# Attention and gated FFN on one core: the last six sections with their loads, splits and gates in another order

## Chip, cores and metric

One core of a Trainium2 chip runs the whole kernel. The metric is the device time of one execution in microseconds (us); a shorter time is better. Times of the profile are counted from the start of the span, which is the time from the first to the last instruction.

## What is computed

A block with attention and a gated FFN on the same normalised input, cut to what matters:

```python
x  = A_x                                  # 1 x 2048 x 576
xn = layernorm(x)
s  = attention(xn, wqkv, 32 heads) @ wo   # the "o" projection comes last
g  = silu((gelu(xn @ w_gate) * (xn @ w_up)) @ w_down)   # hidden size 4608
return x + s * g
```

All data is float32. A product keeps its accuracy by splitting an operand into a high part (rounded to the type that TensorE multiplies fast) and a low part (what is left), so each product is done three times: high by high, high by low, low by high. Making the parts is called a split here.

## The kernel before

**The work.** Tokens are cut into four blocks of 512 (`NB`). The FFN runs block by block in sections: a section makes one chunk of 128 hidden values for the 512 tokens of a block. It multiplies the gate and up weights of the chunk (`gate_up`, L417, 54 matmuls with 512 columns), applies the activation on ScalarE and VectorE, and splits the hidden values (`finish`). Two sections (`G = 2`) share one tile of down weights; after the second of a pair the down weights are split too (`dh`, `dl`), and the two sections that follow each do half of the down products (`down`, L466, 24 matmuls with 288 columns) and add them to Y on VectorE (`add_down`, L455). There are 144 sections; sections 10 to 137 run beside attention. The diff touches the last six, the loop at the end with `n` from 128 to 133. A section is named by this n below.

**The places.** While the last six sections run, the output of attention is projected. A place is 128 tokens (16 places, four to a block). `prepare(p)` splits its normalised attention output (`split_o` on GpSimd, L108, L110, L887) and asks for its rows of `x` and of the stored FFN sum `ys` (`load_xy`, L896 and L898). `load_o` (L876, L877) fetches a block of attention output (1152 KB) into one of two tiles `OT`. `gate_place` makes the silu gate of a place (`gate`: tanh on ScalarE, L424, and one operation on VectorE, L425). `project_o` (L907) makes two products of 14 matmuls, and `put` (L914, L915) multiplies them by the gate, adds `x`, and stores the row of the output (L918). Each of the sections 129 to 132 does three places; two more are projected in section 133 and the last two at the end. For the FFN the last block is finished by `final`.

**What sets the order.** TensorE's order is written out by hand. From the last six sections on, `FF["keep"]` is true and `kept` holds nearly every other instruction to the order in which the program issues it on its engine: VectorE, ScalarE, GpSimd and SP (which starts all DMAs) each run a queue in order, and an instruction that waits holds up what stands behind it. PSUM has three banks under the tag "s"; the products of a section (four of the down sums, six of the places) take them in turn, so a product waits until VectorE has read the product three before it. The rows `xx` and `yy` have four buffers each; while the attention output of the last two heads' groups still has to be normalised (`load_numbers`, `norm_numbers`, L593 to L599), one of the four holds its numbers.

**The loads of weights.** `section` asks for the gate and up weights of the section that follows (`load_gu`, L128) and splits them on GpSimd in three pieces (`split_gu`, tiles `wh`, `wl`, L108 and L110): two before its own products, one behind them in the order of the program. The down weights (L553) are asked for in the second section of a pair, the one whose `finish` splits them on ScalarE (`dh`, L118) and VectorE (`dl`, L119).

Of the kernel before, what the change touches and what calls it, by code (L numbers as in the profile page):

```python
# [8 lines left out]
F32 = mybir.dt.float32  # L9
# [8 lines left out]
P = 128  # L18
NT = S // P
TB = 512  # L20
# [18 lines left out]
G = 2  # L39
# [30 lines left out]
def kernel(ctx: ExitStack, tc: tile.TileContext, x, wqkv, wo, w_gate, w_up, w_down, out):  # L70
# [50 lines left out]
    def raw_tile(shape, pool=wts):  # L121
        return pool.tile(shape, F32, name="raw", tag="raw", bufs=2)
# [278 lines left out]
    def kept(i):  # L401

        if FF["keep"]:
            tc.keep_in_program_order(i)
        return i
# [121 lines left out]
            for j in js:  # L527
                kept(nc.sync.dma_start(ys[b * TB + j * P:b * TB + (j + 1) * P, :], Y[:, j]))

    def section(specials=(), tag="f", raw_d=None):  # L530

        n = FF["n"]
        FF["n"] += 1
        b, r = divmod(n // G, NR)
        g = n % G
        pairs, pg, pu = gate_up(tag)
        if g == 0:
            FF["hs"] = []
        keep = kept
        if asked:  # L540
            xd_last = asked.pop()

            def keep(i):
                no_sync(i, xd_last, "transposed x first")
        nxt = load_gu((n + 1) % (NR * G), keep) if n + 1 < NF else None
        if nxt:
            for k in range(NG - 1):
                first = split_gu(nxt, k, kept)
                if k == 0 and n in ATT and n > ATT.start:
                    no_sync(first, FF["hl"], "hidden values first")  # L550
        if g == G - 1:
            raw = FF["rawd"] = raw_d() if raw_d else raw_tile([P, G, D])
            kept(nc.sync.dma_start(raw, w_down[r * G * P:(r + 1) * G * P, :].rearrange("(g p) n -> p g n", p=P)))  # L553
        for p in spread(pairs, specials):
            p()
        if nxt:
            split_gu(nxt, NG - 1, kept)
        FF["w"] = nxt
        if n + 1 < NF and (n + 1) % (NR * G) == 0:
            FF["xd"] = load_xd(b + 1, FF["key"])  # L560
        FF["act"], FF["rest"] = activate(pg, pu, n < ATT.stop)
        if n < ATT.stop and (n not in ATT or g or not FF["down"] or not FF["down"][0][-2]):
            run_rest()
# [299 lines left out]
    with tc.tile_pool(name="epi", bufs=1, reuse_waits="tile") as epi:  # L863
        AHEAD = 3
        OL = [epi.tile([P, NK, P], F32R, name=f"ol{i}") for i in range(AHEAD)]
        OT = [epi.tile([P, NK, TB], F32, name=f"OT{i}") for i in range(2)]
        OH = [epi.tile([P, NK, P], F32R, name=f"oh{i}") for i in range(AHEAD)]
        S2 = epi.tile([P, 2, D], F32, name="S2")
        OUT = [(k, x, w) for k in range(KT) for x, w in ((0, 0), (0, 1), (1, 0))] + [(KT, 0, 0), (KT, 0, 1)]
        ENDS = NF - len(FIRST)  # L870
        XY = {}

        def load_o(b):

            toks = slice(b * TB, (b + 1) * TB)
            kept(nc.sync.dma_start(OT[b % 2][:, 0:KT, :], oN[0:R0, toks].rearrange("(k p) t -> p k t", p=P)))  # L876
            kept(nc.sync.dma_start(OT[b % 2][0:HR, KT, :], oN[R0:D, toks]))  # L877

        def parts_of(b, j):
            i = (b * TB // P + j) % AHEAD  # L880
            return OH[i], OL[i]

        def split_o(b, j):

            oh, ol = parts_of(b, j)
            split(oh, ol, OT[b % 2][:, :, j * P:(j + 1) * P], kept)
            kept(nc.gpsimd.tensor_copy(oh[HR:P, KT, :], ol[0:HR, KT, :]))  # L887

        def row_tile(name):
            return epi.tile([P, D], F32, name=name, bufs=AHEAD + 1)  # L890

        def load_xy(b, j):

            rows = slice(b * TB + j * P, b * TB + (j + 1) * P)
            xx, yy = XY[b, j] = row_tile("xx"), row_tile("yy")
            kept(nc.sync.dma_start(xx, x[rows, :]))  # L896
            if b < NB - 1:
                kept(nc.sync.dma_start(yy, ys[rows, :]))  # L898

        def gate_place(b, j):  # L900
            yy = XY[b, j][1]
            gate(yy, epi.tile([P, D], F32, name="th"), yy)

        def project_o(b, j, c, tag):
            po = ps.tile([P, TB], F32, name="po", tag=tag, bufs=BANKS[tag])[:, 0:288]
            for i, (k, x_, w) in enumerate(OUT):
                nc.tensor.matmul(po, parts_of(b, j)[x_][:, k, :], OW[w][c][k], start=(i == 0), stop=(i == len(OUT) - 1))  # L907
            return po

        def put(b, j, c, po, add):  # L910

            cc = slice(288 * c, 288 * c + 288)
            xx, yy = XY[b, j]
            kept(nc.vector.scalar_tensor_tensor(yy[:, cc], yy[:, cc], 0.25, po, op0=ALU.mult, op1=ALU.mult))  # L914
            kept(add.tensor_tensor(yy[:, cc], yy[:, cc], xx[:, cc], op=ALU.add))  # L915
            if c or b == NB - 1:
                cc = cc if b == NB - 1 else slice(0, D)
                kept(nc.sync.dma_start(out[b * TB + j * P:b * TB + (j + 1) * P, cc], yy[:, cc]))  # L918

        def cut(hi, lo, raw):  # L920
            split_av(hi, lo, raw, kept)

        places = [(b, j) for b in range(NB) for j in range(TB // P)]

        def prepare(p):

            if p < len(places):
                b, j = places[p]
                split_o(b, j)
                if j == TB // P - 1 and b + 2 < NB:  # L930
                    load_o(b + 2)
                load_xy(b, j)

        for o in OT:
            nc.gpsimd.memset(o[HR:P, KT, :], 0.0)
        load_o(0)
        done = 0
        for n in range(NU * NA, ENDS):
            last = n == ENDS - 1
            section([], "m" if n % 2 else "f",  # L940
                    (lambda: epi.tile([P, G, D], F32, name="raw", tag="raw")) if n > NU * NA + 1 else None)
            if n == NU * NA:
                FF["keep"] = True
                load_wo((n - 1) % KB)
                for p in range(2):
                    prepare(p)
                pieces = [(S2[0:QD * DH, 0, 0:TB], S2[0:QD * DH, 1, 0:TB]), [row_tile(m)[0:QD * DH, 0:TB] for m in ("xx", "yy")]]
                where = [(u % NQ, slice(S - TB, S)) for u in range(NU - 2, NU)]
                for piece, to in zip(pieces, where):
                    load_numbers(*piece, *to)  # L950
                prepare(2)
                load_o(1)
            downs()
            run_rest()
            if n == NU * NA or last:
                finish(epi, cut, 2)
            if n == NU * NA:
                gate_place(*places[0])
            elif not last:
                for i in range(3):  # L960
                    b, j = places[done]
                    for c in range(2):
                        put(b, j, c, project_o(b, j, c, "s"), nc.vector)
                    done += 1
                    if places[done][0] < NB - 1:
                        gate_place(*places[done])
                    if done == 1:
                        for piece, to in zip(pieces, where):
                            norm_numbers(*piece, *to, nc.vector)
                    if i == 0:  # L970
                        finish(epi, cut, 2)
                    prepare(done - 1 + AHEAD)
        for b, j in places[done:done + 2]:
            for c in range(2):
                kept(nc.scalar.activation(S2[:, j, 288 * c:288 * c + 288], project_o(b, j, c, "s"), AF.Copy))
            done += 1
            prepare(done - 1 + AHEAD)

        finals = []

        def final(Y=None, j=None, c=None):

            if finals:
                y, i, d = finals.pop()
                dd = slice(288 * d, 288 * d + 288)
                th = XY[NB - 1, i][1]
                gate(th[:, dd], th[:, dd], y[:, i, dd])
            if Y is not None:
                finals.append((Y, j, c))

        FF["final"] = final
        downs()
        final()
        for j in range(2):
            for c in range(2):
                put(NB - 1, j, c, S2[:, j, 288 * c:288 * c + 288], nc.gpsimd)
        for b, j in places[done:]:
            for c in range(2):
                po = project_o(b, j, c, "mf"[c if j == 3 else 0])
                put(b, j, c, po, nc.vector if j == 3 and c else nc.gpsimd)  # L1000
# [28 lines left out]
```

## Time and profile before

| what | us |
|---|---|
| median of 3 runs | 2572.76 (2571.75 to 2572.87) |
| the profiled execution | 2573.46 |
| its span | 2571.5 |
| TensorE busy | 2548.8 |
| mean granted TensorE clock | 0.997 |

The 1.96 us between the profiled execution and its span lie outside the first and last instruction. In the profile PE is a TensorE matmul and PEld the load of its weights, DVE is VectorE, ACT ScalarE, POOL GpSimd, and SPq the queue of SyncE that starts DMAs. A row of the timeline has the start, the time taken, the engine, the line, the operation, the tiles (output <- inputs), the shape and count, and in brackets how long the engine was idle before and what ended that. A row of the stretches has the time, the busy time of each engine with its instructions, the granted clock of TensorE, the share of DMA time and GB/s. A row of the groups has count, busy time and mean ns of one, and then the idle time before them. A row of the chain has start, time taken and what it was; one that begins with DMA spans from its issue to its landing.

### The profile page before, as it was taken

What the parts mean: (1) busy time and instruction counts of PE and PEld (TensorE: products, weight loads), DVE (VectorE), ACT (ScalarE), POOL (GpSimd) and SP (SyncE); (2) the same over time, 40 slices, a digit from 0 to 9 for tenths busy, and PEclk for the clock granted to TensorE, in tenths of its full rate; (3) what the DMA queues carried; (4) which work ended last, traced back from release to release, by engine and by line L of the source; (5) the groups of instructions that cost most, each with busy time, mean ns of one, the idle gap of its engine ahead of it and who ended that gap; (6) DMA issues with size and microseconds to landing.
All of it is one profiled execution on the core that took longest, in us unless ns stands there. A gap on an engine that the chain in (4) does not pass through costs nothing.

```text
span 2571.5 us, 63350 instructions
## 1 busy us (share of the span) xinstructions
PE 2548.8 (99%) x24038; PEld 1999.7 (78%) x24038; DVE 1949.6 (76%) x3468; ACT 1563.7 (61%) x3114; POOL 1321.4 (51%) x1449
## 2 busy tenths in 40 slices
PE   9999999999999999999999999999999999999988
PEld 8888877777777777777777777777777777777778
DVE  5317978888888888888888888888888888885356
ACT  3223466666666677666666666666776666676512
POOL 2117544555555555554464555555456555445645
PEclk9999999999999999999999999999999999999999
DMA  8866344444464444444465444444436444444463
GB/s 263 271 237 159 93 105 100 104 109 108 107 159 113 111 108 108 105 105 112 112 143 136 108 108 104 110 110 108 110 105 151 110 109 111 109 109 105 119 187 113
DMA packets 391014, 324.99 MB, mean 126 GB/s; under 512 B 108708, under 2 KB 301508, under 8 KB 390712
## 3 DMA queue, kind: packets, MB, share of 16 engines
q1 hardware_dynamic: 390712, 320.95, 47.8%
q8 instruction: 191, 3.13, 0.5%
q14 instruction: 111, 0.91, 0.1%
HBM read 266.10 MB, written 54.19 MB: 125 GB/s over the span
## 4 chain that ended last, share of the span: by engine, by line
PE 95%; DMA 2%; DVE 1%; ACT 1%; POOL 1%; issue 0%; SPq 0%; POOLq 0%; DVEq 0%; ACTq 0%
PE pg L417 29%; PE acc L757 17%; PE py L466 17%; PE pm L687 9%; PE pe L722 9%; PE po L184 7%; PE pu L417 4%; PE po L907 1%; DMA raw<-in_B_w_up_dram 1%; DVE mx L688 1%; ACT pT L723 1%; DMA raw<-in_B_w_down_dram 0%; DMA S<-rT 0%; PE pt L245 0%; POOL wl L110 0%
## 5 line engine op out<-in xcount | busy, mean ns | idle before, releaser
L723 ACT ACTIVATE pT<-pe 128x512 f32<-128x512 f32 x2048 | 1151.0, 598 | 369.5 <-PE pm L687 266.3
L688 DVE TENSOR_REDUCE mx<-pm 128x1 f32<-128x512 f32 x2048 | 1250.1, 682 | 150.6 <-PE pm L687 148.3
L417 PE MATMUL pu<-xd,wh 64*128 64x512 f32 x2592 | 929.9, 391 | 0.0
L417 PE MATMUL pg<-xd,wh 64*128 64x512 f32 x2592 | 929.2, 390 | 0.0
L687 PE MATMUL pm<-KS,q 64*128 64x512 f32 x2048 | 782.7, 388 | 0.0
L722 PE MATMUL pe<-q,KS 64*128 64x512 f32 x2048 | 776.9, 387 | 0.0
L417 PEld LDWEIGHTS pg<-xd,wh 64*128 64x128 f32 x2592 | 477.1, 184 | 119.9 <-issue 30.0
L417 PE MATMUL pu<-xd,wl 64*128 64x512 f32 x1296 | 502.1, 387 | 0.0
L417 PE MATMUL pg<-xd,wl 64*128 64x512 f32 x1296 | 501.6, 387 | 0.0
L417 PEld LDWEIGHTS pu<-xd,wh 64*128 64x128 f32 x2592 | 477.8, 184 | 4.4
L757 PE MATMUL acc<-pT,VS 128*32 128x512 f32 x4096 | 452.8, 594 | 0.0
L110 POOL TENSOR_TENSOR wl<-raw,wh 128x384 fp32r<-128x384 f32 x432 | 435.3, 1020 | 13.7
L687 PEld LDWEIGHTS pm<-KS,q 64*128 64x128 f32 x2048 | 374.8, 184 | 32.7 <-DVE mx L688 3.8
L722 PEld LDWEIGHTS pe<-q,KS 64*128 64x128 f32 x2048 | 370.7, 184 | 24.4
L108 POOL TENSOR_SCALAR hh<-t 128x512 fp32r<-128x512 f32 x128 | 79.1, 618 | 577.2 <-DVE t L444 563.1
L757 PEld LDWEIGHTS acc<-pT,VS 128*32 128x32 f32 x4096 | 127.5, 110 | 289.7 <-issue 278.2
L466 PE MATMUL py<-dh,hh 64*128 64x288 f32 (+1 forms) x2160 | 348.6, 294 | 3.1 <-DVE Y L455 2.1
L466 PE MATMUL py<-dh,hl 64*128 64x288 f32 (+1 forms) x2160 | 346.2, 295 | 0.0
L466 PE MATMUL py<-dl,hh 64*128 64x288 f32 (+1 forms) x2160 | 346.0, 292 | 0.0
L108 POOL TENSOR_SCALAR wh<-raw 128x384 fp32r<-128x384 f32 x432 | 220.5, 521 | 164.8 <-DMA raw<-in_B_w_up_dram 83.1
L455 DVE TENSOR_TENSOR Y<-py,Y 128x288 f32<-128x288 f32 x544 | 226.9, 453 | 65.2 <-PE py L466 61.3
L417 PEld LDWEIGHTS pg<-xd,wl 64*128 64x128 f32 x1296 | 239.1, 184 | 34.4
(121 smaller groups left out, 3082.6 us busy)
## 6 DMA issues: line engine op xcount, KB each, us to landing
KS<-qk SPq DMA_DIRECT2D x1536, 36.0 KB
raw<-in_B_w_gate_dram SPq DMA_DIRECT2D x144, 288.0 KB
raw<-in_B_w_up_dram SPq DMA_DIRECT2D x144, 288.0 KB
raw<-in_B_w_down_dram SPq DMA_DIRECT2D x67, 576.0 KB
VS<-vs SPq DMA_DIRECT2D x128, 152.0 KB
qk<-t SPq DMA_DIRECT2D x72, 256.0 KB
q<-qk SPq DMA_DIRECT2D x384, 36.0 KB
xx<-in_A_x_dram SPq DMA_DIRECT2D x32, 288.0 KB
```

What stands on the lines that cost most here:

```text
L108: first = nc.gpsimd.tensor_scalar(hi, raw, 1.0, 1.0, op0=ALU.mult, op1=ALU.mult)
L110: low_part[:] = [keep(nc.gpsimd.tensor_tensor(lo, raw, f(hi), op=ALU.subtract))]
L184: nc.tensor.matmul(o, st, m, start=(i == 0), stop=(i == len(terms) - 1))
L417: nc.tensor.matmul(o, w[1 + wp][k][rr, c, :], xd[xp][k][rr, c, :], start=(i == 0), stop=(i == len(terms) - 1))
L455: kept(nc.vector.tensor_tensor(yy, py, yy, op=ALU.add))
L466: return nc.tensor.matmul(py, hs[g][a][rr, j * P:(j + 1) * P], wd[w][rr, g, 288 * c:288 * c + 288], start=start, stop=stop)
L687: nc.tensor.matmul(pm, QS[u, r][rr, t * P:(t + 1) * P], KS[(u * NA + c) % KB][r][rr, :], start=True, stop=True)
L688: nc.vector.tensor_reduce(MX[u][:, 2 * r + a, t, c:c + 1], pm, axis=AX.X, op=ALU.max)
L722: nc.tensor.matmul(pe, KS[(u * NA + c) % KB][r][rr, t * P:(t + 1) * P], QS[u, r][rr, :], start=True, stop=True)
L723: nc.scalar.activation(PT[u, kt][:, 2 * r + a, :], pe, AF.Exp, scale=SCALE)
L757: nc.tensor.matmul(ACC[u][32 * a:32 * a + 32, :], VS[(u * NA + c) % VB][:, v:v + 32], pt[:, a, :], start=first, stop=last, skip_group_chec ...
L907: nc.tensor.matmul(po, parts_of(b, j)[x_][:, k, :], OW[w][c][k], start=(i == 0), stop=(i == len(OUT) - 1))
```

## The change

Four things move in the last six sections; no arithmetic changes.

- The down weights are asked for by `next_down`, one section ahead: in 128 behind `load_wo`, and in 130 and 132 behind the gate and up loads. They always go to the tile `raw` of the last stage's pool (the first of the three went to the general weight buffers before).
- In sections 129 to 132 nothing of the gate and up weights is split in `section`; the pieces are split behind the places, two behind the first and one behind the second, each ahead of the `prepare` of that place.
- `gate_place` of a place stands ahead of its own projection, not behind that of the place before. `finish` moves from behind the first place to behind the second, and `norm_numbers` with it.
- `load_o` of block 1 moves from section 128 into 129, behind the gate and up loads; blocks 2 and 3 are asked for with the first place of the block before them (places 4 and 8), not with the last place of the block before that (3 and 7).

```diff
+    def load_down(r, raw):
+        kept(nc.sync.dma_start(raw, w_down[r * G * P:(r + 1) * G * P, :].rearrange("(g p) n -> p g n", p=P)))
+        return raw
...
-    def section(specials=(), tag="f", raw_d=None):
+    def section(specials=(), tag="f", raw_d=None, ahead=True):
...
-            for k in range(NG - 1):
+            for k in range(NG - 1 if ahead else 0):
                 first = split_gu(nxt, k, kept)
...
         if g == G - 1:
-            raw = FF["rawd"] = raw_d() if raw_d else raw_tile([P, G, D])
-            kept(nc.sync.dma_start(raw, w_down[r * G * P:(r + 1) * G * P, :].rearrange("(g p) n -> p g n", p=P)))
+            FF["rawd"] = load_down(r, raw_d() if raw_d else raw_tile([P, G, D])) if ahead else FF.pop("next_d")
         for p in spread(pairs, specials):
             p()
-        if nxt:
+        if nxt and ahead:
             split_gu(nxt, NG - 1, kept)
...
                 split_o(b, j)
-                if j == TB // P - 1 and b + 2 < NB:
-                    load_o(b + 2)
                 load_xy(b, j)
+                if j == 0 and 0 < b < NB - 1:
+                    load_o(b + 1)
+
+        def next_down(n):
+            FF["next_d"] = load_down((len(FIRST) + n) // G % NR, epi.tile([P, G, D], F32, name="raw", tag="raw"))
...
-            section([], "m" if n % 2 else "f",
-                    (lambda: epi.tile([P, G, D], F32, name="raw", tag="raw")) if n > NU * NA + 1 else None)
+            section([], "m" if n % 2 else "f", ahead=n == NU * NA)
             if n == NU * NA:
                 FF["keep"] = True
                 load_wo((n - 1) % KB)
+                next_down(n + 1)
                 for p in range(2):
                     prepare(p)
...
                 prepare(2)
+            elif n == NU * NA + 1:
                 load_o(1)
+            elif n % G == 0:
+                next_down(n + 1)
             downs()
             run_rest()
             if n == NU * NA or last:
                 finish(epi, cut, 2)
-            if n == NU * NA:
-                gate_place(*places[0])
-            elif not last:
+            else:
                 for i in range(3):
                     b, j = places[done]
+                    if b < NB - 1:
+                        gate_place(b, j)
                     for c in range(2):
                         put(b, j, c, project_o(b, j, c, "s"), nc.vector)
                     done += 1
-                    if places[done][0] < NB - 1:
-                        gate_place(*places[done])
-                    if done == 1:
+                    for k in ((0, 1), (2,), ())[i]:
+                        split_gu(FF["w"], k, kept)
+                    prepare(done - 1 + AHEAD)
+                    if i == 1:
+                        finish(epi, cut, 2)
+                    if done == 2:
                         for piece, to in zip(pieces, where):
                             norm_numbers(*piece, *to, nc.vector)
-                    if i == 0:
-                        finish(epi, cut, 2)
-                    prepare(done - 1 + AHEAD)
```

## The prediction, made before the changed kernel ran

> **What bounds the kernel now.** I read the page's busy times first, then the stretches of the last sections, then the timeline of each engine there, and last the chain of waits. The page says that TensorE does nearly all of the time:
>
> ```profile
> PE 2548.8 (99%) x24038; PEld 1999.7 (78%) x24038; DVE 1949.6 (76%) x3468; ACT 1563.7 (61%) x3114; POOL 1321.4 (51%) x1449
> ```
>
> Against a span of 2571.5 us, all its idle time is 22.7 us, so only a change in what leaves it idle can pay. I call a section by the n of the last loop (128 to 133). Cut at the first gate-and-up matmul of sections 129 to 133, the stretches are:
>
> ```profile
> core 0: us, PE busy (x) PEld busy (x) DVE busy (x) ACT busy (x) POOL busy (x), PEclk, DMA share, GB/s
> 2433.68:2463.66 29.98, 22.73 (x164) 20.82 (x163) 17.98 (x28) 5.49 (x8) 16.73 (x17) 0.90 0.76 180
> 2463.66:2487.12 23.46, 21.36 (x163) 19.88 (x163) 14.26 (x24) 4.38 (x7) 12.64 (x15) 0.99 0.73 227
> 2487.12:2515.88 28.76, 22.38 (x164) 20.62 (x163) 15.77 (x24) 4.68 (x7) 16.18 (x17) 0.88 0.60 175
> 2515.88:2536.71 20.83, 20.83 (x163) 19.29 (x162) 16.26 (x23) 3.33 (x6) 16.95 (x19) 1.00 0.46 130
> ```
>
> All four do the same matmuls; section 132 does them in 20.83 us without a gap, and that is the floor. The others lose 9.15, 2.63 and 7.93 us, 19.71 us together. TensorE's timeline shows three waits in them:
>
> ```profile
> 2460.00 0.85 PE L907 MATMUL po<-KS,oh 128*128 128x288 f32 x2 [7.25 <-DVE yy L914]
> 2475.02 0.41 PE L466 MATMUL py<-dh,hh 128*128 128x288 f32 x1 [2.10 <-DVE Y L455]
> 2512.54 0.85 PE L907 MATMUL po<-KS,oh 128*128 128x288 f32 x2 [6.38 <-DVE yy L914]
> ```
>
> The first and third wait for a PSUM bank that `put` of a place has yet to read. VectorE and ScalarE show why it was late, and why the second was:
>
> ```profile
> 2456.45 1.16 ACT L118 ACTIVATE dh<-raw 128x1152 fp32r<-128x1152 f32 x1 [10.41 <-DMA raw<-in_B_w_down_dram]
> 2457.65 1.94 DVE L119 TENSOR_TENSOR dl<-raw,dh 128x1152 fp32r<-128x1152 f32 x1 [6.98 <-ACT dh L118]
> 2459.51 0.44 DVE L914 SCALAR_TENSOR_TENSOR yy<-yy,po 128x288 f32<-128x288 f32 x1
> 2472.53 0.68 ACT L424 ACTIVATE th<-yy 128x576 f32<-128x576 f32 x1 [14.34 <-DMA yy<-ys]
> 2473.24 0.76 DVE L425 SCALAR_TENSOR_TENSOR yy<-th,yy 128x576 f32<-128x576 f32 x1 [7.45 <-ACT th L424]
> ```
>
> In section 129 the split of the down weights stands in VectorE's queue ahead of `put` of the second place, and it waits for a load asked for in the same section. In 130 the gate of place 3, queued at the end of 129, waits for its row of `ys` ahead of the four Y sums. So each loss is a load that came late, with in-order work queued behind it.
>
> **The clock.** The 19.71 us is more than the three waits, 15.73 us. Where the rest went:
>
> ```profile
> 2440.00:2452.50 12.50, 12.50 (x96) 12.44 (x94) 8.01 (x15) 2.44 (x4) 4.45 (x5) 1.00 1.09 218
> 2452.50:2460.00 7.50, 0.26 (x2) 0.02 (x1) 2.31 (x3) 1.74 (x2) 4.56 (x5) 0.83 0.33 110
> 2460.00:2470.00 10.00, 10.00 (x68) 8.91 (x68) 5.59 (x8) 0.00 (x0) 9.40 (x9) 0.79 0.45 123
> 2470.00:2480.00 10.00, 7.90 (x59) 7.39 (x56) 5.27 (x11) 3.01 (x5) 0.33 (x2) 1.00 0.94 292
> ```
>
> Behind the 7.25 us wait the granted clock is 0.79; behind the one of 2.10 us it stays at 1.00. Matmuls after a long wait are slow for a while, so a removed long wait returns some 2.0 us more than its length ((19.71 - 15.73) / 2). The Trainium skill, "TensorE: Matmul & The Clock Gate", section "Why this matters for your kernels", says to leave no idle gap over about 3 us; both waits here agree. By it a remainder of 3 us in one gap would cost some 2.0 us more than below, in short ones nothing.
>
> **The change part by part.**
>
> *Down weights.* Sections 128, 130 and 132 now ask for the weights of 129, 131 and 133. For 129 the request follows `load_wo` on SP, for 131 the gate and up loads of 130. What SP and DMA did there before:
>
> ```profile
> 2416.27 1.05 SPq L629 DMA_DIRECT2D KS<-wos  x2
> 2428.28 0.54 SPq L799 DMA_DIRECT2D rT<-rec  x1
> 2428.92 0.40 SPq L876 DMA_DIRECT2D OT<-oN  x1
> 2421.70:2428.90 7.20, 7.20 (x68) 4.62 (x62) 4.04 (x2) 0.00 (x0) 6.47 (x9) 1.00 0.09 22
> 2443.13 3.52 SPq L553 DMA_DIRECT2D raw<-in_B_w_down_dram  x1
> 2438.44 0.70 POOL L887 CAST oh<-ol 64x128 fp32r<-64x128 f32 x1
> 2443.35 0.43 PE L907 MATMUL po<-KS,oh 128*128 128x288 f32 x2
> ```
>
> DMA is idle from 2421.7 to 2428.9 (share 0.09), so 576 KB at 218 to 292 GB/s, 2.0 to 2.7 us, fits in ahead of the blocks. At worst, held by a buffer of the attention stage until rT is stored, it goes with the block at 2428.92 and delays that by 2.7 us; the first place, prepared by 2439.1 now (the cast above), is then ready before 2442, and TensorE takes it at 2443.35. Either way it lands some 15 us ahead of its split. Waits one and three go.
>
> *Gates at their place.* The same twelve gates, each now behind the Y sums instead of ahead of them, so wait two goes. In exchange the gate of place 0 moves from 128 into 129: 0.8 to 2.1 us of VectorE before the first `put`, and the banks that `put` frees are first needed by the fourth product, 3 x 1.85 us after the first began (six take 11.09 us, below). That cover of 5.5 us hides it, so I cost it at nothing; without the cover it would be 2.1 us.
>
> *Weights split behind places.* This is the step that can cost. The three splits for the next section ran first on GpSimd; now two run ahead of the section's first prepared place and the third behind it. The prices:
>
> ```profile
> L110 POOL TENSOR_TENSOR wl<-raw,wh 128x384 fp32r<-128x384 f32 x432 | 435.3, 1020 | 13.7
> L108 POOL TENSOR_SCALAR wh<-raw 128x384 fp32r<-128x384 f32 x432 | 220.5, 521 | 164.8 <-DMA raw<-in_B_w_up_dram 83.1
> L110 POOL TENSOR_TENSOR wl<-raw,wh 128x384 fp32r<-128x384 f32 x3 | 4.1, 1359 | 0.3
> L108 POOL TENSOR_SCALAR wh<-raw 128x384 fp32r<-128x384 f32 x3 | 2.4, 802 | 10.0 <-DMA raw<-in_B_w_up_dram 10.0
> L110 POOL TENSOR_TENSOR ol<-OT,oh 128x640 fp32r<-128x640 f32 x16 | 27.0, 1689 | 1.3
> L108 POOL TENSOR_SCALAR oh<-OT 128x640 fp32r<-128x640 f32 x16 | 13.7, 858 | 16.6 <-PE po L907 9.2 <-DMA OT<-oN 6.5
> L887 POOL CAST oh<-ol 64x128 fp32r<-64x128 f32 x16 | 6.7, 417 | 1.0
> ```
>
> A split costs 1.54 us over the whole kernel (1020 + 521) and 2.16 in section 130 (1359 + 802), where VectorE is busy too; a prepared place 2.96. So the third split ends 3 x 1.54 + 2.96 = 7.6 to 9.5 us after the up weights land. TensorE wants it two thirds through the gate-and-up part:
>
> ```profile
> 2522.32 3.38 PE py L466 x24
> 2525.69 11.09 PE po L907 x84
> ```
>
> That part is 2515.88 to 2522.32, 6.44 us, so two thirds are 4.3 us into the section. No wait arises if the up weights land 3.3 to 5.2 us before the section starts.
>
> *Blocks a place later.* This moves loads on SP. The landings of before:
>
> ```profile
> 2441.77 13.28 DMA raw<-in_B_w_up_dram
> 2493.39 5.75 DMA OT<-oN
> 2499.16 9.65 DMA raw<-in_B_w_down_dram
> ```
>
> For section 130: the up weights landed at 2455.05, behind block 1 (1152 KB, 5.4 us at 218 GB/s). Now they stand ahead of it: 2449.6. The section starts at 2433.68 + 20.83 = 2454.5; the lead is 4.9, so a wait of 0 to 0.3 us.
>
> For 131: the `yy` of place 3 must take the buffer of place 0, since the last numbers hold the spare one until after place 1. So SP stands until the first output block is stored, about 2456, behind block 1. Then come `yy`, output, `xx`, `yy`, block 2, two stores of numbers, output, `xx`, `yy`, gate and up: 4032 KB, 14.1 us at 292 GB/s, from 2457, so 2471.1. The start is 2475.3, the lead 4.2: 0 to 1.0 us.
>
> For 132: gate and up stand behind block 3, which waits for place 7's split: 3 splits and 2 places after 2471.1, 10.5 to 12.4 us, 2481.6 to 2483.5; block 3 took 5.75 us from its second request, and gate and up add 576 KB, 2 us: 2489.5 to 2491.5 with the request. The start is 2496.2: a lead of 4.7 to 6.7, 0 to 0.5 us.
>
> *Sum.* -19.71, and 0 to 1.8 back from these. The sections now run packed, as only 132 did, and its rows show what that does to VectorE:
>
> ```profile
> L425 DVE SCALAR_TENSOR_TENSOR yy<-th,yy 128x576 f32<-128x576 f32 x3 | 5.8, 1934 | 0.0
> L915 DVE TENSOR_TENSOR yy<-yy,xx 128x288 f32<-128x288 f32 x6 | 5.2, 859 | 0.2
> ```
>
> A gate of 0.76 us above takes 1.93 here. Section 132 still ran without a gap, but GpSimd's steps stretch likewise, so I take 3.0 us back. The Trainium skill, "SBUF — State Buffer", section "SBUF: two separate sides", has VectorE and GpSimd exclude one another for a whole instruction where VectorE reads two SBUF operands; the rows agree. By that alone I would take all splits at 2.16 us or more and give back about 5.
>
> The profiled execution took 2573.46 us: 2573.46 - 19.71 + 3.0 = 2556.75. It lies 0.70 over the median of 2572.76, so I forecast 2556.0. What this kernel's timing can tell from no change is about 0.2%, 5 us.
>
> **The rivals.**
>
> *Weights late at the head of the section.* If SP's chain in 129 (store, `yy`, block, store of numbers, `xx`, gate, up) runs at the 227 GB/s of section 130 instead of 292, its 4032 KB take 18.2 us and 131's weights land 4 us later: a wait of 3.2 to 5.1 us, say 4, and 2.0 of slow clock. Block 3, gate and up at that rate add 1.9 us in 131 and leave 132 a wait of up to 2. For it: 218 GB/s with DMA saturated. Against: 292 where it worked through such a mix. Time: 2556.0 - 3.0 + 8 = 2561.
>
> *The request is held.* The early load's buffer lies over the attention stage's, and if SP gets to it only behind the blocks, loss one stays: 2556 + 9.15 = 2565. Against: the idle DMA above.
>
> *Slower.* The chain from SP through GpSimd becomes the bound: the first split waits for weights that land after the section starts, and 131, 132 and 133 each wait. To give back 19.71 us and 5 more, three waits of 6.3 us with 2.0 of slow clock each (24.9) are needed, so up weights landing 1.1 to 3.0 us behind the section's start (6.3 + 4.3 less 7.6 to 9.5). It would take a further block of 1152 KB, 4 to 5.4 us, ahead of the gate and up loads in each section, since the leads above are 4 to 7 us. GpSimd's 16.95 us of 20.83 in section 132 speaks for little slack, its 4 us of slack against a lasting lag. Time: 2578.
>
> **How the numbers follow.** Forecast 0.68, weights late 0.13, request held 0.07, no change in sum 0.04, slower 0.08. Faster 0.88, same 0.04, slower 0.08. The low end is all of 19.71 back and no wait, 2553.0, with 0.5 of scatter: 2552.5. The high end takes in both faster rivals: 2566.
>
> **What the changed profile would show.** The early down load requested before 2431 and no wait for it on ScalarE; no wait of TensorE on a bank that `put` reads over 1 us; the granted clock at 1.00 through sections 129 to 132; each of them 20.8 to 23 us; gates on VectorE behind the Y sums; TensorE's remaining waits on GpSimd's `wl`, on the third split of a section, under 3 us. I am wrong if a section begins with a wait of over 3 us for `wl`, if SP stands on the early load while the first blocks wait, or if VectorE's longer queue makes products wait for banks.

## The result and the profile after

The changed kernel takes 2561.03 us (median of 6 runs, 2558.55 to 2563.50), the one before 2572.38 us in the same comparison (6 runs, 2571.45 to 2574.04): a ratio of 0.9955 with a 95% interval of 0.9942 to 0.9968, so 11.35 us less. The forecast was 2556.0 us in a range of 2552.5 to 2566.0. The profiled execution took 2561.06 us with a span of 2559.2.

TensorE's busy row on the page of the changed kernel:

```profile
PE 2545.9 (99%) x24038; PEld 1982.6 (77%) x24038; DVE 1945.4 (76%) x3468; ACT 1563.6 (61%) x3114; POOL 1320.7 (52%) x1449
```

Its idle time is 13.3 us of the span, where it was 22.7. The stretches of sections 129 to 132, cut in the same way (time, busy time of each engine, granted clock, DMA share, GB/s):

```profile
2434.59:2455.44 20.85, 20.85 (x163) 19.29 (x162) 13.76 (x24) 5.39 (x8) 10.18 (x11) 1.00 1.00 252
2455.44:2480.39 24.95, 22.25 (x164) 19.15 (x163) 15.92 (x28) 3.70 (x6) 15.31 (x17) 1.00 0.88 237
2480.39:2503.18 22.79, 21.44 (x165) 19.24 (x164) 13.56 (x22) 4.76 (x7) 15.64 (x19) 1.00 0.71 209
2503.18:2524.44 21.26, 21.11 (x163) 19.21 (x162) 16.67 (x25) 3.70 (x6) 17.72 (x19) 1.00 0.53 158
```

The granted clock is 1.00 in all four. Section 129 is at the floor; 130 is 4.1 us over it, 131 2.0 and 132 0.4: 6.5 us are given back, where 3.0 were forecast. TensorE's timeline shows where, always at a gate-and-up matmul that waits for a split of GpSimd:

```profile
2459.18 0.49 PE L417 MATMUL pg<-xd,wl 64*128 64x512 f32 x1 [0.58 <-POOL wl L110]
2462.75 0.50 PE L417 MATMUL pg<-xd,wh 64*128 64x512 f32 x1 [1.46 <-POOL wh L108]
2463.83 0.50 PE L417 MATMUL pg<-xd,wl 64*128 64x512 f32 x1 [0.58 <-POOL wl L110]
2485.54 0.50 PE L417 MATMUL pg<-xd,wh 64*128 64x512 f32 x1 [0.77 <-POOL wh L108]
2507.93 0.49 PE L417 MATMUL pg<-xd,wl 64*128 64x512 f32 x1 [0.15 <-POOL wl L110]
```

The waits of 7.25, 2.10 and 6.38 us are gone. The split of the down weights on ScalarE has no wait ahead of it any more, and the gate stands on VectorE (the second fence) right ahead of the rows of its own place; `dl` and `norm_numbers` (L601) follow behind the section's second place:

```profile
2448.04 1.15 ACT L118 ACTIVATE dh<-raw 128x1152 fp32r<-128x1152 f32 x1
```

```profile
2449.02 0.75 DVE L425 SCALAR_TENSOR_TENSOR yy<-th,yy 128x576 f32<-128x576 f32 x1
2453.32 1.66 DVE L119 TENSOR_TENSOR dl<-raw,dh 128x1152 fp32r<-128x1152 f32 x1
2454.91 1.50 DVE L601 TENSOR_TENSOR S<-S 72x512 f32<-72x512 f32 x1
```

SP's queue (start, length of the issue) shows the loads in their new order; L531 is the early request for down weights, L879 and L880 are blocks:

```profile
2430.29 0.51 SPq L880 DMA_DIRECT2D OT<-oN  x1
2430.92 0.50 SPq L531 DMA_DIRECT2D raw<-in_B_w_down_dram  x1
...
2442.55 0.63 SPq L128 DMA_DIRECT2D raw<-in_B_w_up_dram  x1
2443.51 0.38 SPq L879 DMA_DIRECT2D OT<-oN  x1
...
2456.67 0.32 SPq L901 DMA_DIRECT2D yy<-ys  x1
```

And the chain that leads to the waits of 130 and 131 (start, length, what; a DMA row runs from its issue to its landing):

```profile
2433.10 9.43 DMA yy<-ys
...
2442.55 10.54 DMA raw<-in_B_w_up_dram
...
2453.27 0.52 POOL wh L108
2453.79 0.07 issue
2453.86 1.99 POOL wl L110
2455.85 2.20 POOL wh L108
2458.05 0.07 issue
2458.13 1.00 POOL wl L110
2459.13 0.91 POOL oh L108
2460.03 0.07 issue
2460.11 1.65 POOL ol L110
2461.76 0.02 issue
2461.78 7.53 DMA OT<-oN
...
2469.32 8.58 DMA raw<-in_B_w_up_dram
```

Four things are to be seen. The up weights of 130 took 10.54 us from issue to landing, 2453.09. The two splits that follow took 5.8 us together (2453.27 to 2459.13) instead of 3.1. And block 2 could not be asked for until the split of place 3 (`ol`, ended 2461.76) had read the tile that it overwrites; the up weights of 131 went out only when that block had landed, and landed themselves at 2477.90. And SP's requests wait for earlier transfers: that of the up weights of 130 went out as the `ys` row of place 1 landed (2433.10 + 9.43 = 2442.53), that of the up weights of 131 as the first part of block 2 landed (2461.78 + 7.53 = 2469.31), and in both cases SP had asked for that transfer exactly eight requests earlier. So transfers in flight put off the next request here. What sets the eight is open; no run varied it.

### The profile page after: what moved, and what is told of

Read it like the earlier page. It is cut to its first block, busy times and chain, and to the rows that moved or that the text cites. A ratio compares the mean times of both kernels' runs of the same rounds, so it can differ in the third digit from the quotient of the medians.

```text
span 2559.2 us, 63348 instructions
## 1 busy us (share of the span) xinstructions
PE 2545.9 (99%) x24038; PEld 1982.6 (77%) x24038; DVE 1945.4 (76%) x3468; ACT 1563.6 (61%) x3114; POOL 1320.7 (52%) x1449
## 4 chain that ended last, share of the span: by engine, by line
PE 95%; DMA 2%; POOL 1%; ACT 1%; DVE 1%; issue 0%; SPq 0%; POOLq 0%; ACTq 0%; DVEq 0%
PE pg L417 30%; PE acc L760 18%; PE py L466 17%; PE pm L690 9%; PE pe L725 9%; PE po L184 7%; PE pu L417 3%; DMA raw<-in_B_w_up_dram 1%; PE po L910 1%; ACT pT L726 1%; POOL wl L110 0%; DMA yy<-ys 0%; PE pt L245 0%; DMA OT<-oN 0%; POOL ol L110 0%; POOL wh L108 0%
```

## The experiments

Single executions of one kernel scatter by 2 to 7.5 us, partly ahead of section 129: it starts anywhere from 2431.05 to 2435.83 in the profiles, 2433.68 before and 2434.59 after. So the lengths of sections 129 to 132 in the profile are the finer measure; they were 103.04 us before and 89.87 after, over a floor of 4 x 20.83 = 83.32. Lengths and sums are rounded and can differ by up to 0.02 from the rows shown. All edits but the first are to the changed kernel, or to the experiment named.

| kernel | median us | ratio to before, 95% | 129, 130, 131, 132 | sum |
|---|---|---|---|---|
| before | 2572.38 | 1 | 29.98, 23.46, 28.76, 20.84 | 103.04 |
| changed | 2561.03 | 0.9955, 0.9942 to 0.9968 | 20.86, 24.95, 22.79, 21.27 | 89.87 |
| only the down weights early | 2564.69 | 0.9970, 0.9960 to 0.9980 | 22.97, 31.75, 20.82, 20.82 | 96.36 |
| blocks back | 2567.10 | 0.9977, 0.9968 to 0.9986 | 22.38, 25.38, 24.06, 25.55 | 97.37 |
| gates back | 2561.59 | 0.9961, 0.9949 to 0.9974 | 20.90, 27.53, 20.84, 22.27 | 91.54 |
| free buffer | 2560.00 | 0.9954, 0.9941 to 0.9968 | 20.86, 23.44, 21.99, 21.28 | 87.57 |
| three splits together | 2558.72 | 0.9946, 0.9933 to 0.9958 | 20.86, 24.65, 21.68, 21.11 | 88.30 |
| block 1 later | 2558.49 | 0.9946, 0.9931 to 0.9962 | 20.86, 25.84, 21.07, 21.73 | 89.50 |
| all blocks later | 2558.66 | 0.9945, 0.9931 to 0.9959 | 20.86, 25.96, 20.83, 20.82 | 88.47 |
| three together, free buffer | 2556.58 | 0.9941, 0.9929 to 0.9953 | 20.86, 24.10, 23.34, 20.82 | 89.12 |
| the same, block 1 later | 2555.63 | 0.9934, 0.9922 to 0.9947 | 20.86, 22.69, 23.37, 20.82 | 87.74 |
| the same, all blocks later: "all three edits" | 2553.61 | 0.9928, 0.9914 to 0.9943 | 20.86, 20.82, 20.82, 20.82 | 83.32 |
| all three edits, stage buffer again | 2554.40 | 0.9925, 0.9910 to 0.9940 | 20.86, 21.09, 20.82, 20.82 | 83.58 |
| all three edits, gates back | 2554.16 | 0.9923, 0.9906 to 0.9939 | 20.86, 22.35, 20.82, 20.82 | 84.85 |

### What the parts of the change are worth

**Only the down weights early** (the kernel before, with the requests of one part of the change):

```diff
+                next_down(n + 1)
...
+            elif n % G == 0:
+                next_down(n + 1)
```

The first request stands in 128, behind `load_wo`, the second in 130 and 132.

> The kernel before with the early requests for down weights alone. If that request is the whole gain, the two long waits on `put` go and nothing replaces them: 2553 to 2557 us, and the rest of the change costs time. If the order of the loads is needed too, section 130 begins with a wait of 3 to 5 us for its up weights, which land behind block 1, and the gate of place 3 still holds up the Y sums for 2 us: 2560 to 2566 us.

It took 2564.69 us. The waits one and three go, but the wait on Y grows. TensorE's timeline:

```profile
2458.18 0.49 PE L417 MATMUL pg<-xd,wh 64*128 64x512 f32 x1 [2.05 <-POOL wh L108]
2475.40 0.61 PE L466 MATMUL py<-dh,hh 128*128 128x288 f32 x1 [5.76 <-DVE Y L455]
```

The up weights of 130 land behind block 1, 21.9 us into section 129; before it was 21.4, but then 130 started 7 us later. And TensorE waits longer on Y behind the gate of place 3, which is still queued a section early on VectorE and waits for its row of `ys`: 5.76 us instead of 2.10. 10.24 us of half clock follow these two waits in 130. So this part alone brings 6.7 us in the sections (103.04 - 96.36) of the 17.1 that 129 and 131 had lost (9.15 + 7.93), and the rest goes into 130, which takes 31.75 us. The other parts are what lets the gain through.

**Blocks back** (everything changed but the block loads):

```diff
+                if j == TB // P - 1 and b + 2 < NB:
+                    load_o(b + 2)
...
-                if j == 0 and 0 < b < NB - 1:
-                    load_o(b + 1)
...
-            elif n == NU * NA + 1:
-                load_o(1)
```

with block 1 asked for in 128 again.

> The changed kernel with the three block loads back at their old places. Theory (the up weights of 130 must be ahead of block 1): they land at about 2457 us as in e1, the third split ends at 2465 to 2467 where TensorE wants it at 2459.7, and the clock halves: sections 129 to 132 take 93 to 96 us instead of 89.9, 2564 to 2567 us. Rival (the order of the blocks is worth little): 2560 to 2562 us.

It took 2567.10 us, and 97.37 us in the sections, 7.5 more than the changed kernel and over the 93 to 96 expected. Its stretches:

```profile
2457.68:2483.06 25.38, 21.81 (x162) 19.19 (x163) 13.72 (x27) 3.81 (x6) 12.68 (x15) 1.00 0.77 222
2483.06:2507.12 24.06, 23.02 (x162) 20.41 (x162) 11.80 (x22) 4.76 (x7) 12.38 (x15) 0.93 0.66 198
2507.12:2532.67 25.55, 23.24 (x162) 20.37 (x162) 14.59 (x23) 3.70 (x6) 21.98 (x25) 0.93 0.51 151
```

Every section from 130 on now loses 3.2 to 4.7 us. The up weights land at the heads of their sections, and waits of 1.46, 1.30 and 0.38 us stand there, with 1.1 us for the third split behind them in 130 and 132. This is the prediction's slower rival in small: with a block ahead of gate and up in each section the chain from SP through GpSimd does become the bound, at a price of 4 us a section and not of 8.3 (24.9 / 3).

**Gates back**, first in the changed kernel, and last in the kernel with the three edits below:

```diff
-                    if b < NB - 1:
-                        gate_place(b, j)
...
+                    if places[done][0] < NB - 1:
+                        gate_place(*places[done])
```

> The changed kernel with the gates back behind the place before. If the row of place 3 now lands before the Y sums of section 130 anyway (2459.9 against 2466.6 us), the move of the gates is worth nothing: 2560 to 2562 us. If the move is what removed the second wait, 2.1 to 2.6 us come back: 2563 to 2564 us.

The wait on Y does not come back: 2561.59 us. A wait of 2.17 us for the third split of 130 and 6.83 us of half clock behind it make 130 longer and 131 shorter, so this run leaves the gates' own worth open; TensorE's wait for GpSimd may have given VectorE the time it needed. Where nothing else waits, it shows:

> The kernel with all three edits (free buffer, three splits together, every block behind the first `put` of a section), with the gates put back behind the place before. Theory (the gates' place is worth nothing of itself; what made the wait of 2.10 us was a row of `ys` that landed late, and with the blocks asked for later the rows land in time): no wait of over 0.5 us for a Y sum, sections 129 to 132 within 0.5 us of 83.3 us in all, and the time within 1.5 us of 2553.6. Rival (the gate still ends up waiting for its row ahead of the Y sums): a wait of 1 us or more on `py`, and the four sections at 85 us or more.

The four sections took 84.85 us against 83.32, all in 130. TensorE's timeline and, in the second fence, VectorE's:

```profile
2464.96 0.40 PE L466 MATMUL py<-dh,hh 128*128 128x288 f32 x1 [1.26 <-DVE Y L455]
```

```profile
2461.83 2.12 DVE L425 SCALAR_TENSOR_TENSOR yy<-th,yy 128x576 f32<-128x576 f32 x1
2463.86 0.68 DVE L431 SCALAR_TENSOR_TENSOR t<-t,pg 128x512 f32<-128x512 f32 x1
```

So I had the mechanism wrong, and the rival had it half right: there is a wait on Y, but no row came late. VectorE is behind with its work beside GpSimd's splits (the gate takes 2.12 us instead of 0.75), and the gate stands ahead of the Y sums. The gates' place is worth 1.5 us by itself here.

### Where the 6.5 us went

**Free buffer.** The first early down load goes to a general weight buffer:

```diff
-            FF["next_d"] = load_down(..., epi.tile([P, G, D], F32, name="raw", tag="raw"))
+            raw = raw_tile([P, G, D]) if n == NU * NA + 1 else epi.tile([P, G, D], F32, name="raw", tag="raw")
+            FF["next_d"] = load_down(..., raw)
```

> The changed kernel with the first early down load in a general weight buffer, which is free long before. Theory (the early load went into the busy stretch and delays the up weights of 130): it is asked for at about 2418 us and lands by 2424; the up weights of 130 land some 2.5 us earlier, the wait of section 130 falls from 4.1 to about 1.6 us: 2558 to 2559 us. Rival (stretched splits set the wait): 2560.5 to 2561.5 us.

The load is asked for at 2417.26 instead of 2430.92, ahead of block 0. Its chain, to be held against that of the changed kernel:

```profile
2431.61 7.88 DMA yy<-ys
...
2439.50 10.58 DMA raw<-in_B_w_up_dram
...
2450.86 1.02 POOL wl L110
2451.87 0.70 POOL wh L108
```

Counted from the start of section 129 the up weights of 130 land at 16.55 us instead of 18.50. The transfer took as long as before, 10.58 and 10.54 us; its request went out 2 us earlier, 5.97 us into 129 instead of 7.96, because the row of `ys` that it follows landed earlier (2431.61 + 7.88 = 2439.49). All profiles agree: with the stage buffer, and gate and up ahead of block 1, the request comes 7.84 to 8.81 us into 129 (six profiles), with the free buffer 5.83 to 6.88 (five). The splits, now early enough to miss the long operations of VectorE, take 1.02 and 0.70 us instead of 1.99 and 2.20. Section 130 falls from 24.95 to 23.44 us; what is left there are waits of 1.36 and 0.66 us for the third split, behind a place whose `ol` took 3.16 us. The median moves by 1 us, less than the scatter of single runs, and lies between the times of theory and rival.

**Three splits together**, ahead of the prepared place:

```diff
-                    for k in ((0, 1), (2,), ())[i]:
+                    for k in ((0, 1, 2), (), ())[i]:
```

> The changed kernel with all three splits ahead of the first prepared place. Theory (the third split is late because it stands behind a place on GpSimd): the wait of section 130 falls from 4.1 us to 1 to 2, that of 131 from 2.0 to under 0.5, that of 132 goes; 2561.0 becomes 2556 to 2557 us. Rival (VectorE and GpSimd hold each other up, so the splits stretch wherever they stand): 2560 to 2562 us.

The wait for the third split goes, but GpSimd shows a first split that is stretched from its start, and TensorE waits 1.83 us for it:

```profile
2452.57 1.56 POOL L108 TENSOR_SCALAR wh<-raw 128x384 fp32r<-128x384 f32 x1 [8.59 <-DMA raw<-in_B_w_up_dram]
2454.22 2.58 POOL L110 TENSOR_TENSOR wl<-raw,wh 128x384 fp32r<-128x384 f32 x1
```

Section 130 gains 0.3 us, 131 1.1. One wait took the place of another, with 3.41 us of half clock behind it, and the median of 2558.72 us lies between the two expected.

**Block 1 later**, and **all blocks later**: each block asked for behind the first `put` of a section, so that gate and up go ahead of it. The old requests of the blocks concerned go; with block 1 alone the new line reads `if done == 1: load_o(1)`:

```diff
                     done += 1
+                    if i == 0 and done <= 7:
+                        load_o(done // 3 + 1)
```

> The changed kernel with block 1 asked for behind the first `put`, some 5 us later. Theory (block 1, though asked for behind the up weights of 130, takes DMA time from them): they land by 2451 us instead of 2453.1, section 130 takes 23 us instead of 24.95. Rival (only what is queued ahead of them counts): they land at 2453, section 130 takes 25 us.

> The changed kernel with one edit: each attention block (1, 2 and 3) asked for behind the first `put` of sections 129, 130 and 131; the splits stay two and one around the second place, and the early down weights stay in the buffer of the attention stage. Theory (loads and split order are separate terms): the wait of 131 for its weights goes, and that of 130 falls as the up weights land earlier (2449 to 2450.5 rather than 2453.1), but the third split behind a place leaves up to 2.3 us and a spell of half clock in 130: 86.5 to 89 us for the four sections, 2555.5 to 2558. Rival (the order of the blocks is the whole of it): within 1 us of the run with all three edits.

With block 1 alone moved the up weights of 130 land 17.34 us into section 129 (18.50 in the changed kernel), yet 130 takes 25.84 us: the third split stands behind the prepared place, its wait is 2.34 us, and 3.41 us of half clock follow. The theory was right that block 1 puts off the landing and wrong on what that is worth in 130. With all three blocks moved it is the same in 130 (25.96), and 131 and 132 are at the floor, 20.83 and 20.82. So in 130 the third split behind a place is a second term. What the order of the blocks is worth in 131 isn't settled by this run: a long 130 alone also brought 131 to the floor (20.82 with only the down weights early, 20.84 with gates back, both without this edit). The last of the edits together settles it. The wait in the run with all blocks moved:

```profile
2462.01 0.49 PE L417 MATMUL pg<-xd,wh 64*128 64x512 f32 x1 [2.45 <-POOL wh L108]
```

**The edits together.** Three splits and free buffer; then block 1 later as well; then all blocks later:

> The changed kernel with the three splits together and the first down load in the free buffer. If the late weights and the split behind a place are all that is left over the floor: the splits of 130 run from 2450.3 to about 2456, ahead of TensorE in every piece; sections 129 to 132 take 84 to 85 us, 2555 to 2557 us. If the splits stretch against VectorE wherever they stand: section 130 still takes over 23 us, the four over 87 us, 2558 to 2560 us.

> e7 with block 1 asked for behind the first `put` as well. If block 1 takes DMA time from the up weights, they land at about 2448.5 us and nothing is left to win: within 0.5 us of e7 in the four sections, unless the later block 1 makes places 4 and 5 late, which would show as a wait of TensorE on `ol` in section 130.

> The kernel with the first down weights in a free buffer, the three splits together behind the first place, and now each attention block (1, 2 and 3) asked for behind the first `put` of sections 129, 130 and 131, so that the gate and up loads of 131 and 132 no longer stand behind blocks 2 and 3. Theory (what is left over the floor of 83.3 us in sections 129 to 132 is weights that land late because loads asked for ahead of them share the DMA engines): the up weights of 131 land some 3 us earlier than in the run before (2476.2 there, so about 2473), no wait at the head of 131, no half clock, and the four sections take 84 to 85 us: 2552 to 2554 in all. Rival (the chain on SP sets it, whatever the order of the blocks): the up weights of 131 land within 1 us of 2476, a wait of 1.5 to 2 us and the half clock stay, and the four take 87 us or more, 2555 or more. A second rival: the blocks themselves now come late and the place that takes the first rows of a block waits for them: a wait of over 2 us on `ol` in a product.

In the first two 130 has no wait of its own, but the up weights of 131 come late: waits of 2.93 and 1.80 us at the head of 131, each with 3.41 us of half clock in 131. The second was expected within 0.5 us of the first and took 1.4 us less in the sections. In the third the weights of 131 land at 2467.5 and nothing waits. Its stretches:

```profile
2434.30:2455.16 20.86, 20.86 (x164) 19.30 (x163) 15.02 (x23) 5.38 (x8) 12.86 (x14) 1.00 0.89 223
2455.16:2475.98 20.82, 20.82 (x164) 19.30 (x163) 16.34 (x27) 3.70 (x6) 19.68 (x19) 1.00 0.86 253
2475.98:2496.80 20.82, 20.82 (x164) 19.29 (x163) 15.75 (x24) 4.76 (x7) 14.16 (x16) 1.00 0.70 212
2496.80:2517.62 20.82, 20.82 (x164) 19.29 (x163) 17.29 (x25) 3.70 (x6) 14.57 (x16) 1.00 0.72 215
```

All four sections are at the floor. At 2553.61 us (2552.08 to 2557.17) it has the lowest median of the kernels here and is faster than both the kernel before and the changed one (2558.55 to 2563.50 above). The two variants of it in the last rows of the table can't be told from it by their times alone, only by their sections. GpSimd is as busy in 130 as anywhere, 19.68 us of 20.82, and its splits are still stretched (the third `wl` for 130 took 2.60 us); only the lead covers them.

**Stage buffer again**, in that kernel:

> The kernel with all three edits, with the first down weights put back into the buffer of the attention stage, so that they go behind block 0 again. Theory (that costs the up weights of 130 some 2.3 us, which comes out of the lead): they land at about 2452.4 where section 130 starts at 2455.2, a lead of 2.8 us; the three splits together then end at 2457.0 to 2459.0, wanted at 2459.5, so a wait of 0 to 1 us in 130 and nothing in 131 and 132: 83.3 to 84.5 us for the four sections, 2553 to 2555.5. Rival (the splits stretch as in the run with three splits alone): a wait of 1.5 us or more in 130 with a spell of half clock, 86 us or more, 2556 or more.

The up weights of 130 are asked for 7.84 us into 129 instead of 5.87 and land 1.4 us later (17.1 us against 15.7), and 130 takes 21.09 us instead of 20.82. So the load behind block 0 delays the landing here too, but it costs TensorE only 0.27 us, because the lead isn't spent elsewhere.

## Why the prediction was right, and where its sum was off

**What bounds the kernel: right.** The three waits were loads that came late with in-order work behind them, and with those loads early, and the gates behind the Y sums, they are gone. Section 129 gave back all of its 9.15 us, and the early request alone already removes the first and the third wait.

**The clock: right in its effect.** With the long waits gone the clock is 1.00 in all four sections, and the slow matmuls behind them are gone as well. The Trainium skill, "TensorE: Matmul & The Clock Gate", section "Why this matters for your kernels", puts the limit at an idle gap of about 3 us; the runs here differ: a gap of 1.83 us was followed by half clock (last section).

**Down weights: the effect right, the place wrong.** I expected the request in the idle DMA time before 2428.9, and named the bound that it goes with the block. The bound is what happened (2430.92, behind both parts of block 0). What I missed is the price at that bound: not the first place, which was ready, but the up weights of 130, whose request waits for rows that stand behind the early load. The free buffer takes 1.95 us off their landing, all of it by the earlier request.

**Gates at their place: right.** The gate of place 0 moved in at no cost, section 129 being at the floor. The wait that it removes is real even without late rows, 1.26 us.

**Weights split behind places: the term that was mis-sized.** 3.0 us were forecast to come back, 6.5 did in the profile. The other 0.9 between 2556.75 and 2561.06 is the later start of section 129 (2434.59 instead of 2433.68), which varies from profile to profile; with one profile of each kernel it stays open whether the change has a part in it. Of the signs named, one failed: section 130 took 24.95 us and not 20.8 to 23. The term fails in three places:

- The landing in 130. Forecast 15.9 us after the start of 129 (2449.6 - 2433.68), measured 18.50. For the place ahead of block 1 I took 5.4 us off the old landing, which leaves 7.8 us from the old request (2441.77) to 2449.6. The request came hardly earlier, 7.96 us into 129 against 8.09 before, and the landing 10.54 us behind it (13.28 before). With the free buffer the landing is 16.55, with block 1 moved 17.34, with both 15.7. Block 1, asked for 1 us after the up weights, is in flight with them.
- The price of a split. I bounded it by 2.16 us for a pair of steps, a mean over three. Where VectorE runs `dl` and `norm_numbers` beside it, one pair took 2.51 (0.52 + 1.99) and the next 3.20 (2.20 + 1.00), and in the run with three together 4.14 (1.56 + 2.58). The third split ended 10.7 us after the landing (2463.8), not 7.6 to 9.5. The Trainium skill, "SBUF — State Buffer", section "SBUF: two separate sides", has a VectorE operation with two SBUF operands and a GpSimd one that reads SBUF hold each other up for a whole instruction; the trace agrees (`wl` of 1.99 us beside `dl` of 1.66, against 1.02 in the run where it is earlier), and its sum, 5 us given back, was nearer than mine.
- The landing in 131. Forecast 16.6 us into 130, measured 22.5. The first store held SP until 2456.67, as I had it (2456 to 2457). From there I summed 4032 KB at 292 GB/s, 14.1 us, and it took 21.2. SP stood for 5.8 us of that: 2.7 for the `yy` of place 4 until the row of place 1 was stored (2460.64), 0.8 for block 2 until the split of place 3, behind two stretched splits on GpSimd, had read its tile (2461.78), and 2.3 for the up weights until the first part of block 2 had landed (2469.32). I used the first rule for place 3 and the second for block 3, and left them out here; the third I didn't know.

For 132 the lead was 5.2 us (2498.03 to 2503.18), inside the 4.7 to 6.7 forecast, and its wait 0.15.

**The rivals.** "Weights late at the head of the section" gave 2561, what was measured, and its late landing in 131 is there. But it put 4 us of wait and half clock at the head of 131; it was 2.0 us in all there and 4.1 in 130, with the clock at 1.00, so its number fits in part by luck. "The request is held" came true as a place, not as a price: loss one did not stay. "Slower" needed a block ahead of gate and up in each section; with the blocks put back this is what happens, at half the price that I gave it.

## What to carry to other kernels

When several in-order queues feed one engine, taking away the waits that the profile names moves the bound to the loads behind them: reckon the landing of every load that follows, with the transfers in flight beside it, with the instruction that frees its buffer and with what the issuing queue waits for ahead of the request, and give what is wanted first a lead over what is wanted later. A split that must end inside a section is priced at its longest row beside the other engine's work, not at its mean. Here the order of three loads, of one split and of one buffer was worth another 6.5 us in the sections, and of it one edit at a time showed 0.4 to 2.3 us.

## What the runs showed of the hardware that I had not expected

**The clock changes on a grid.** Apart from the start and the end of the kernel the spells of half clock last 3.41 or 6.83 us in the traces, and two spells of one execution start whole multiples of 3.41 us apart: 2460.37 and 2474.02 with only the down weights early (13.65 = 4 x 3.41), 2485.21 and 2515.93 with the blocks back (30.72 = 9 x 3.41). Cut on that grid, with a spell for its origin, the stretches show which waits cost clock. Before, around the wait of 2.10 us:

```profile
2471.04:2474.46 3.42, 1.88 (x15) 1.65 (x13) 1.22 (x2) 1.17 (x2) 0.00 (x0) 1.00 1.04 408
2474.46:2477.87 3.41, 2.85 (x21) 2.85 (x22) 2.94 (x7) 1.21 (x2) 0.00 (x0) 1.00 1.11 299
```

With the free buffer:

```profile
2457.41:2460.82 3.41, 1.86 (x14) 0.96 (x12) 2.80 (x5) 0.00 (x0) 3.17 (x4) 1.00 0.47 120
2460.82:2464.24 3.42, 2.95 (x22) 2.32 (x23) 0.16 (x1) 0.60 (x1) 3.18 (x5) 1.00 0.93 278
```

With block 1 later:

```profile
2457.61:2461.02 3.41, 1.81 (x14) 1.28 (x16) 0.22 (x1) 0.00 (x0) 3.15 (x5) 1.00 0.69 184
2461.02:2464.44 3.42, 3.42 (x17) 2.68 (x14) 0.94 (x2) 1.24 (x3) 3.18 (x4) 0.50 0.99 272
```

A window with TensorE busy for 1.86 or 1.88 us was followed by full clock, one with 1.81 by half. In sections 129 to 132 of all 14 profiles, busy times of up to 1.82 us in a window at full clock were followed by half clock, and of 1.86 or more by full. So a wait of 2.10 us across two windows cost nothing more than itself, and one of 1.83 us inside one window (three splits together, 1.58 us busy) cost 3.41 us at half clock. Short waits in one window add up: with three splits together, the free buffer and block 1 later, the last 0.95 us of the wait of 1.80 us and a wait of 0.66 us behind it fell into one window with 1.82 us busy, and half clock followed. At the end of the kernel the same limit doesn't hold. In the run with all blocks later as its only edit:

```profile
2552.14:2555.55 3.41, 1.60 (x13) 1.37 (x11) 1.16 (x3) 0.00 (x0) 2.08 (x3) 1.00 0.60 207
2555.55:2558.96 3.41, 0.00 (x0) 0.00 (x0) 0.00 (x0) 0.00 (x0) 0.00 (x0) 1.00 0.13 45
```

A window with 1.60 us was followed by full clock there, so the busy time of one window isn't the whole rule; what else counts is open. The Trainium skill's page on TensorE named above has, in its section "Part 1: The HAM clock gate (the "warmup" mystery)", a free-running window of 3413 ns; the grid agrees. The limit inside the window is read from the traces of these sections alone, and no run varied a wait on purpose to find it.

**Transfers of one queue overlap.** The up weights of 130 took 10.54 us from issue to landing with block 1 asked for right behind them, 9.14 with that block later. Over the profiles with the stage buffer it was 9.81 to 10.54 us (three) against 9.14 to 9.28 (three), with the free buffer 10.58 to 11.24 (two) against 8.37 to 10.21 (three): block 1 costs about 1 us. In section 130 of the fastest kernel, with less in flight around them, those of 131 took 5.69.
